# First rounds in another order, adapter loads and products later, a new warm-up and another last unit, in a retention-plus-adapters kernel

## The chip, the cores and the metric

The kernel runs on one core of one Trainium2 chip. A core has a matrix engine (TensorE, PE in the profile, its weight loads PEld), VectorE (DVE), ScalarE (ACT), GpSimd (POOL) and SyncE (SP), which work side by side and wait for each other through semaphores; transfers between the chip's main memory and the on-chip memory go through 16 DMA engines and are issued from an engine's queue, here mostly SP's. The metric is the device time of one execution in microseconds (us).

## The reference

The first half is a retention layer: attention scores without a softmax, weighted by a decay that depends on the distance and cut to the past. The second is a mixture of adapters on its output: each token picks the two best of eight experts, and their low-rank products are added.

```python
# q, k, v: (8 batches, 8 heads, 576 positions, 64), float32
scores = (1/sqrt(64)) * q @ k.T
rel = pos[:, None] - pos[None, :]
ret = scores * where(rel >= 0, gamma[h] ** rel, 0)       # gamma[h] = 1 - 2**(-5 - h)
x = (ret @ v).transpose(0, 2, 1, 3).reshape(4608, 512)

logits = x @ w_gate                                      # (4608, 8)
topk = the 2 largest logits of each token
w = softmax over those 2
out = x + sum over the 2: w * ((x @ A[e]) @ B[e])        # A: 512 x 16, B: 16 x 512
```

## The kernel before

**Units.** The 576 positions are cut into chunks of 128, with a last one of 64. A unit is one chunk of two batches (four batches for the last chunk): units 0 to 15 are full, four for each of four chunks, and 16 and 17 hold the last chunk. Units 0 to 3 belong to the first chunk and have no state from an earlier one. Within a unit, positions come as two blocks of 64 ("t = 0, 1"). From unit 2 to 15 ("paired"), q is loaded in another layout with longer runs.

**The decay** is split: k is multiplied by gamma to the power of minus its position and q by gamma to the power of its position times the scale (`scale_`, lines 162 to 184), on GpSimd, on VectorE, or half each. What is left of the mask is a 0/1 triangle, which `masks` (line 279) multiplies in while copying the scores out, four instructions for a unit in an order that is a parameter.

**Stages of a unit**, by the names that the order below uses, with the engine's lines:
- turn: `stage_T` and `evict_T` transpose k and q on TensorE (lines 215, 202) and copy the result out on ScalarE (240, 235). `shift_q` copies q's halves to the other partitions (252, 253).
- sums: `stage_U` forms k-transposed times v (300), `stage_A` adds it to the running state SP (332 to 335), `put` or `put_state` copies the state beside v (316).
- scores: `stage_S` (269) and the four masks (289). The first-chunk units copy only one half of q.
- products: `stage_X` multiplies masked scores, and q, with v, and with the state (350). In the first chunk the first half of it uses only the first 64 rows. `evict_x` copies the result, xT, out on ScalarE (366, 371).
- logits: `stage_Z` multiplies xT with AW, which holds A and w_gate (393), and copies to zs (406). choose: `routing_2` finds the best two on VectorE (416 to 421). `routing_3` is the sigmoid on ScalarE (431), which is the softmax over two. `routing_4` weights the small products on GpSimd (441, 443), into zc.
- small: `stage_P` and `evict_z` transpose zc (378, 386). back: `stage_B` transposes xT back (459). output: `stage_Y` adds the product with B (475), `evict_o` copies out (492), `store` writes.

**Order.** It is written out by hand: on each engine instructions run in the order in which the program issues them, and semaphores hold each one until its data and its buffer are ready. Loads are issued on SP's queue, units 0 to 5 ahead of everything, the later ones in `ahead(t)`, which also issues due stores, and, on GpSimd, copies the state for unit t + 1 and scales k and q of unit t + 2. Units 0, 1 and 2 run through their first stages one after the other (lines 575 to 628); then come rounds by hand (796 to 845), in which logits of unit 0 begin; from round 5 a loop (847) does scores(t), logits(t-1), small(t-2), choose(t-1), sums(t+1), turn(t+1), back(t-2), products(t), output(t-2). `finish` (693) handles the last units. Before, the order of the first units by hand on TensorE is, with the unit's number: ... scores 1, products 1, turn 2, sums 2, scores 2, logits 0, products 2, turn 3, sums 3, scores 3, logits 1, small 0, back 0, products 3, output 0, turn 4, logits 2, sums 4, scores 4, logits 3, small 1 and 2, back 1, output 1, sums 5, turn 5, back 2, products 4, output 2.

**Fills.** `fill_small` and `fill` run matmuls on zeros, ahead of the first data and where TensorE would wait in units 0 and 1.

**The adapter.** AW is loaded by four transfers of A and one of w_gate between the loads of unit 2 and unit 3 (lines 555 to 563), in runs of 64 and 32 bytes.

Of the kernel before, what the change touches and what calls it, by code (L numbers as in the profile page):

```python
# [18 lines left out]
def kernel(  # L19
# [115 lines left out]
    def load(u, w):  # L135
# [9 lines left out]
        elif w == "v":  # L145
            for t in range(2):
                hf = slice(64 * t, 64 * t + 64)
                nc.sync.dma_start(  # L148
                    out=block(u, t)[hf], in_=rows(w, 2 * bp, 2, s0 + 64 * t, 64)
                )  # L150
# [209 lines left out]
    def evict_x(u):  # L360
        st[u]["xT"] = []
        for b in range(2):
            xt = mo.tile([128, HP, 128], FP32, tag=f"xT{b}", name=f"xT{b}", bufs=3)
# [130 lines left out]
    def fill_small(n):  # L494
        pf = [pp.tile([128, 96], FP32, tag=f"o{r}", name=f"pf{r}") for r in range(2)]
        for _ in range(n):
            for c in range(2):
                for r in range(2):
                    sl = slice(64 * r, 64 * r + 64)
                    nc.tensor.matmul(  # L500
                        pf[r][64 * c : 64 * c + 64],
                        lhsT=zero[sl, 0:64],
                        rhs=zero[sl, 0:96],
                        start=True,
                        stop=True,
                        skip_group_check=True,
                    )

    def fill(n):
        if n == 0:  # L510
            return
        pf = pp.tile([128, 512], FP32, tag="o1", name="pf")
        for _ in range(n):
            nc.tensor.matmul(
                pf, lhsT=zero[:, 0:128], rhs=zero, start=True, stop=True, skip_group_check=True
            )

    o3 = out.rearrange("(b s) m -> b s m", s=S)

    def store(u):  # L520
        c, bp = units[u]
        of = st.pop(u)["osb"].rearrange("p b a o d -> p b (a o d)")
        for b in range(2):
# [4 lines left out]
            else:  # L528
                for t in range(2):
                    (nc.gpsimd if b and u == NU - 2 else nc.sync).dma_start(  # L530
                        out=o3[4 * bp + 2 * t + b, 128 * c : 128 * c + 64, :],
                        in_=of[64 * t : 64 * t + 64, b],
                    )


    def load_batch(u, w, b):
# [3 lines left out]
        )  # L540

# [13 lines left out]
    for dt in range(HP):  # L555
        nc.sync.dma_start(  # L556
            out=AW[:, dt, 0:ER].rearrange("p (e r) -> p e r", e=E),
            in_=moe_A[:, 128 * dt : 128 * dt + 128, :].rearrange("e d r -> d e r"),
        )
    nc.sync.dma_start(  # L560
        out=AW[:, :, ER : ER + E],
        in_=moe_w_gate.rearrange("(t p) e -> p t e", p=128),
    )
    for u in range(3, 6):
        for w in "kqv":
            load(u, w)

    both = (nc.gpsimd, nc.vector)
    pool2 = (nc.gpsimd, nc.gpsimd)
    dve2 = (nc.vector, nc.vector)  # L570
# [4 lines left out]
    fill_small(20)  # L575
# [8 lines left out]
    by_t = ((0, 0), (0, 1), (1, 0), (1, 1))  # L584
    for b, w, n in ((0, "k", 2), (0, "q", 1), (1, "k", 1), (1, "q", 0)):
        stage_T(0, w, (b,), "u" if w == "q" else "x")
        evict_T(0, w, b)
        fill(n)
# [24 lines left out]
    masks(1)  # L613
    scale_(2, "k", both)
# [12 lines left out]
    masks(2)  # L627
    scale_(3, "k", pool2)

    def ahead(t):  # L630
# [5 lines left out]
        if has(t + 1):  # L636
            first_state(t + 1)
        if has(t + 2):
            scale_(t + 2, "k", pool2)
            if t > 2:  # L640
                scale_(t + 2, "q", pool2)
# [51 lines left out]
    def finish():  # L693
# [16 lines left out]
        pz, zs, zc, po, osb = [], [], [], [], []  # L710
# [7 lines left out]
        for b in range(2):  # L718
            z = mo.tile([128, ER + E], FP32, tag=f"ze{b}", name="ze", bufs=1)
            m8 = mo.tile([128, E], FP32, tag=f"m8e{b}", name="m8e", bufs=1)  # L720
            ns = mo.tile([128, 1], FP32, tag=f"nse{b}", name="nse", bufs=1)
            ge = mo.tile([128, E], FP32, tag=f"gee{b}", name="gee", bufs=1)
            sg = mo.tile([128, E], FP32, tag=f"sge{b}", name="sge", bufs=1)
            cm = mo.tile([128, E], FP32, tag=f"cme{b}", name="cme", bufs=1)
            c = mo.tile([128, ER], FP16, tag=f"zce{b}", name="zce", bufs=1)
# [9 lines left out]
            )  # L735
            nc.scalar.activation(
                out=sg, in_=z[:, ER : ER + E], func=AFT.Sigmoid, bias=ns, scale=2.0
            )
            nc.gpsimd.tensor_tensor(out=cm, in0=ge, in1=sg, op=ALU.mult)
            nc.gpsimd.tensor_tensor(  # L740
                out=c.rearrange("p (e r) -> p e r", e=E),
                in0=z[:, 0:ER].rearrange("p (e r) -> p e r", e=E),
# [3 lines left out]
            zc.append(c)  # L746
            if b == 0:
                small(u - 1, "x0")
        back(u - 1)
        stage_Y(u - 1)  # L750
        evict_o(u - 1, (nc.scalar, nc.vector))
        store(u - 1)

        def small_b(b):
            p = pp.tile([128, 128], FP16, tag=f"u{b}", name="pzte")
            nc.tensor.matmul(
                p, lhsT=zc[b], rhs=ident16, is_transpose=True, start=True, stop=True
            )
            zt = mo.tile([128, 128], FP16, tag=f"zTe{b}", name="zTe", bufs=1)
# [3 lines left out]
        def output_b(b, zt):  # L763
            o = mo.tile([128, HP, 2, 64], FP32, tag=f"oe{b}", name="oe", bufs=1, align_bytes=256)
            for ho, eng in ((0, nc.scalar), (1, nc.vector)):
# [8 lines left out]
            of = o.rearrange("p a o d -> p (a o d)")  # L774
            for t in range(2):
                (nc.scalar if b and t else nc.sync).dma_start(
                    out=o3[4 * qd + 2 * t + b, 128 * c : 128 * c + 64, :],
                    in_=of[64 * t : 64 * t + 64],
                )

        zt0 = small_b(0)
# [119 lines left out]
```

## Time and profile before

| what | value |
|---|---|
| three runs | 190.16, 190.33, 191.59 us; median 190.33 |
| profiled execution | 190.79 us, of which the span of the profile is 188.9 us |
| TensorE busy | 167.3 us (89% of the span) |
| VectorE, ScalarE, GpSimd busy | 113.3, 114.1, 108.7 us |
| mean granted TensorE clock | 0.986 |
| moved by DMA | 38.99 MB, mean 206 GB/s |

A row of a timeline reads: start, length, engine, line, operation, output and inputs, count, and in brackets the engine's idle time before it with what ended it. An "issue" there is a wait for nothing that the profile can name. A row of the windows view gives, for a stretch of time, each engine's busy time with the count of instructions, then the granted clock of TensorE (1.00 is full), the share of time in which the DMA engines were busy, and GB/s. A row of the chain gives start, length, engine and tile. Rows of groups give busy time, mean length in ns, and idle time ahead of them.

### The profile page before, as it was taken

The page shows a single profiled execution, that of the slowest core. Times are in us where ns is not written, and L with a number is a line of the kernel's source. Part 1 is how long each engine was busy: PE and PEld are TensorE (multiplying, and loading weights), DVE is VectorE, ACT ScalarE, POOL GpSimd, SP SyncE. Part 2 cuts the span into 40 slices and gives each one's busy share as a digit, 9 for nine tenths or more (in the row PEclk, how much of TensorE's full clock was granted, in tenths as well). Part 3 has the DMA queues.
Part 4 walks back from the last instruction along what each step waited for, and adds up shares of the span by engine and source line. Part 5 has one row for each costly group of instructions (what it writes and reads, how often), then busy time and mean ns, then how long its engine had stood idle before and what let it go on. Part 6 is the DMA issues. An engine that isn't in the chain of part 4 may idle for free.

```text
span 188.9 us, 10441 instructions
## 1 busy us (share of the span) xinstructions
PE 167.3 (89%) x4675; PEld 148.9 (79%) x4675; DVE 113.3 (60%) x227; ACT 114.1 (60%) x255; POOL 108.7 (58%) x162
## 2 busy tenths in 40 slices
PE   3989598799889889898999999999997999999960
PEld 3578498588879788788999989899996988988840
DVE  1384837665296475748577787777594846555240
ACT  3437163735569484765767868494959394674650
POOL 1333321567769988493949586675969397520240
PEclk9999969999999999999999999999999999999998
DMA  7999969999999999999999999999998853112325
GB/s 157 248 221 225 227 70 232 202 224 246 224 228 235 262 252 277 252 260 247 241 257 246 266 232 250 221 278 226 271 206 243 181 169 115 50 68 111 115 56 166
DMA packets 108075, 38.99 MB, mean 206 GB/s; under 512 B 88768, under 2 KB 103488, under 8 KB 108032
## 3 DMA queue, kind: packets, MB, share of 16 engines
q1 hardware_dynamic: 107568, 37.71, 81.1%
q8 instruction: 36, 0.59, 1.4%
q0 software_dynamic: 240, 0.39, 1.0%
q10 hardware_dynamic: 224, 0.24, 0.5%
q14 instruction: 7, 0.06, 0.1%
HBM read 29.02 MB, written 9.44 MB: 204 GB/s over the span
## 4 chain that ended last, share of the span: by engine, by line
PE 59%; SPq 14%; issue 7%; DMA 6%; POOL 5%; DVE 4%; ACT 2%; POOLq 0%; ACTq 0%
PE px L350 15%; PE pz L393 12%; PE ps_s L269 8%; PE pu L300 6%; PE po L475 5%; PE po L459 4%; PE pt_k L215 4%; SPq L148 3%; SPq L556 3%; PE pt_q L202 3%; DMA k<-in_k_dram 3%; SPq L160 3%; DMA q<-in_q_dram 3%; POOL k L179 2%; SPq L538 2%
## 5 line engine op out<-in xcount | busy, mean ns | idle before, releaser
L179 POOL TENSOR_TENSOR k<-k,pack 128x512 f32<-128x512 f32 x32 | 34.9, 1109 | 17.4 <-DMA k<-in_k_dram 16.5
L350 PE MATMUL px<-x,v 128*64 128x64 f32 (+1 forms) x576 | 39.3, 226 | 2.6 <-DVE x L289 0.8
L289 DVE TENSOR_TENSOR x<-ps_s,pack 64x512 f32<-64x512 f32 (+1 forms) x38 | 25.1, 660 | 25.9 <-PE ps_s L269 25.6
L350 PE MATMUL px<-qT,v 128*64 128x64 f32 (+1 forms) x576 | 39.2, 226 | 1.3 <-DVE qT L289 1.1
L350 PEld LDWEIGHTS px<-x,v 128*64 128x64 f32 (+1 forms) x576 | 36.2, 140 | 4.4 <-ACT kT L240 1.0
L350 PEld LDWEIGHTS px<-qT,v 128*64 128x64 f32 (+1 forms) x576 | 36.1, 140 | 1.9 <-DVE qT L289 1.2
L393 PE MATMUL pz<-AW,xT 128*128 128x136 f32 x272 | 36.1, 286 | 0.6 <-ACT kT L240 0.6
L393 PEld LDWEIGHTS pz<-AW,xT 128*128 128x128 f32 x272 | 32.6, 190 | 1.8 <-ACT kT L240 0.8
L169 POOL TENSOR_TENSOR qs<-q,pack 128x512 f32<-128x512 f32 x25 | 26.1, 1062 | 4.1 <-DMA q<-in_q_dram 4.1
L406 ACT COPY zs<-pz 128x272 f32<-128x272 f32 x17 | 6.6, 386 | 33.2 <-PE pz L393 32.5
L289 DVE TENSOR_TENSOR qT<-ps_s,pack 64x512 f32<-64x512 f32 (+1 forms) x38 | 25.1, 660 | 1.1
L269 PE MATMUL ps_s<-qT,kT 64*64 64x64 f32 x1152 | 23.6, 224 | 2.1 <-issue 1.4
L269 PEld LDWEIGHTS ps_s<-qT,kT 64*64 64x64 f32 x1152 | 20.4, 137 | 6.2 <-issue 3.1
L441 POOL TENSOR_TENSOR cm<-ge,sg 128x16 f32<-128x16 f32 x17 | 4.0, 234 | 36.5 <-PE pt_k L215 16.9
L316 POOL COPY v<-SP 64x512 f32<-64x512 f32 x32 | 20.5, 640 | 1.6
L300 PE MATMUL pu<-v,k 64*64 64x64 f32 x1024 | 19.2, 221 | 0.8 <-DMA v<-in_v_dram 0.8
L240 ACT COPY kT<-pt_k 128x512 f32<-128x512 f32 x34 | 18.2, 589 | 1.2 <-PE pt_k L215 1.0
L253 DVE COPY x<-qT 64x512 f32<-64x512 f32 x17 | 14.5, 852 | 7.4 <-ACT qT L235 5.0
L366 ACT COPY xT<-px 128x512 f32<-128x512 f32 x28 | 16.3, 625 | 4.4 <-PE px L350 4.4
L300 PEld LDWEIGHTS pu<-v,k 64*64 64x64 f32 x1024 | 16.9, 134 | 2.5 <-DMA v<-in_v_dram 0.9
L492 ACT COPY osb<-po 128x512 f32<-128x512 f32 x33 | 17.6, 584 | 1.0 <-PE po L475 1.0
L252 DVE COPY x<-qT 64x512 f32<-64x512 f32 x14 | 8.1, 579 | 16.0 <-ACT qT L235 12.0
(68 smaller groups left out, 242.6 us busy)
## 6 DMA issues: line engine op xcount, KB each, us to landing
v<-in_v_dram SPq DMA_DIRECT2D x36, 256.0 KB, 5.2
q<-in_q_dram SPq DMA_DIRECT2D x34, 256.0 KB, 5.2
out_dram<-osb SPq DMA_DIRECT2D x32, 256.0 KB, 4.2
k<-in_k_dram SPq DMA_DIRECT2D x15, 512.0 KB, 5.7
k<-in_k_dram SPq DMA_DIRECT2D x6, 256.0 KB, 4.3
q<-in_q_dram SPq DMA_DIRECT2D x1, 512.0 KB, 6.9
out_dram<-oe SPq DMA_DIRECT2D x3, 128.0 KB, 3.3
AW<-in_moe_A_dram SPq DMA_DIRECT2D x4, 64.0 KB, 3.6
```

The lines of the kernel that those rows point to most:

```text
L169: engines[b].tensor_tensor(out=qs[:, :, 4 * b : 4 * b + 4, :].rearrange("p e h d -> p h e d"), in0=tl[:, b * H : b * H + H, :].rearrange(" ...
L179: engines[b].tensor_tensor(out=tl[:, b * H : b * H + H, :], in0=tl[:, b * H : b * H + H, :], in1=g[:, c, :].unsqueeze(2).broadcast_to((128 ...
L240: nc.scalar.copy(out=tl[:, r], in_=st[u]["p" + w][r])
L253: eng.tensor_copy(out=x2[0:64, 1, b], in_=qT[64:128, 1, b])
L269: nc.tensor.matmul(ps[ho][64 * t : 64 * t + 64, b, hp, :], lhsT=kT[sl, t, b, hp, :], rhs=qT[sl, t, b, hp, :], start=(hp == 0 and b == bs[0 ...
L289: nc.vector.tensor_tensor(out=out, in0=in0, in1=m, op=ALU.mult)
L300: nc.tensor.matmul(pu[t][64 * ho : 64 * ho + 64, b, hp, :], lhsT=kn[sl, h, :], rhs=block(u, t)[sl, h, :], start=(hp == 0 and b == 0), stop ...
L316: copy(out=dst[:, :, :, ho, :], in_=src[64 * ho : 64 * ho + 64])
L350: nc.tensor.matmul(px[b][64 * ho : 64 * ho + 64, hp, t, :], lhsT=block(u, t)[rw, b * H + 2 * hp + ho, :], rhs=facing(u, t, ho)[rw, b, hp, ...
L366: nc.scalar.copy(out=xt.rearrange("p a (t i e) -> p (a t) e i", t=2, e=2), in_=px.rearrange("p a t (e i) -> p (a t) e i", e=2),)
L393: nc.tensor.matmul(pz[:, b, :], lhsT=st[u]["xT"][b][:, dt, :], rhs=AW[:, dt, :], start=(dt == 0), stop=(dt == HP - 1), skip_group_check=True,)
L492: copy(out=s["osb"][:, :, :, ho, :], in_=s["po"][ho])
```

## The change

- The small quadrant matmuls of the warm-up become 64 matmuls over the whole array (`warmup`), and the fills are cut into narrower pieces (256 or 128 columns, the same number of columns in all).
- Unit 3's k, q and the first half of its v are loaded ahead of the adapter; the first transfer of A comes next, then the second half of that v, then the other four.
- The masks of units 1, 2 and 3 run in the order `by_t`, first half of the positions first. Fills of 4 and 2 (in units of 512 columns) stand ahead of products 1 and 2. k of unit 2 is scaled on GpSimd alone, k of unit 4 half on VectorE.
- Unit 3 runs through its first stages as units 1 and 2 do; logits 0 come only then. TensorE's order becomes: ... scores 1, fill, products 1, turn 2, sums 2, scores 2, fill, products 2, turn 3, sums 3, scores 3, logits 0, products 3, k of turn 4, q of turn 4, logits 1, small 0, back 0, output 0, sums 4, scores 4, logits 2, small 1, back 1, output 1, products 4, logits 3, small 2, turn 5, sums 5, back 2, output 2, and then the same loop. xT gets four buffers in place of three.
- In `finish`, the weighting of unit 17 moves from GpSimd to VectorE, its two batches are interleaved in another way with unit 16's output, which VectorE alone now copies out, while ScalarE copies out unit 17's; the stores of the last chunk go out as one transfer for each batch of a pair (of two blocks, 256 KB) in place of two.

```diff
-    def load(u, w):
+    def load(u, w, ts=(0, 1)):
...
-            for t in range(2):
+            for t in ts:
...
-            xt = mo.tile([128, HP, 128], FP32, tag=f"xT{b}", name=f"xT{b}", bufs=3)
+            xt = mo.tile([128, HP, 128], FP32, tag=f"xT{b}", name=f"xT{b}", bufs=4)
...
+    def warmup(n):
+        pf = pp.tile([128, 512], FP32, tag="o1", name="pf")
         for _ in range(n):
+            nc.tensor.matmul(
+                pf[:, 0:64], lhsT=zero[:, 0:128], rhs=zero[:, 0:64], start=True, stop=True,
...
+    def fill(n, w=256):
...
+        for _ in range(512 * n // w):
+                pf[:, 0:w], lhsT=zero[:, 0:128], rhs=zero[:, 0:w], start=True, stop=True,
...
-                for t in range(2):
-                    (nc.gpsimd if b and u == NU - 2 else nc.sync).dma_start(
-                        out=o3[4 * bp + 2 * t + b, 128 * c : 128 * c + 64, :],
-                        in_=of[64 * t : 64 * t + 64, b],
-                    )
+                nc.sync.dma_start(
+                    out=o5[bp, b, :, 128 * c : 128 * c + 64, :], in_=of[:, b]
+                )
...
+    def load_adapter(dt):
+        if dt < HP:
+            nc.sync.dma_start(
+                out=AW[:, dt, 0:ER].rearrange("p (e r) -> p e r", e=E),
...
+        else:
+            nc.sync.dma_start(
+                out=AW[:, :, ER : ER + E],
...
-    for dt in range(HP):
-        nc.sync.dma_start(
-            out=AW[:, dt, 0:ER].rearrange("p (e r) -> p e r", e=E),
...
-    nc.sync.dma_start(
-        out=AW[:, :, ER : ER + E],
...
-    for u in range(3, 6):
+    for w in "kq":
+        load(3, w)
+    load(3, "v", (0,))
+    load_adapter(0)
+    load(3, "v", (1,))
+    for dt in range(1, HP + 1):
+        load_adapter(dt)
+    for u in range(4, 6):
         for w in "kqv":
             load(u, w)
...
-    fill_small(20)
+    warmup(64)
...
-        fill(n)
+        fill(n, 128)
...
-    masks(1)
-    scale_(2, "k", both)
+    masks(1, None, by_t)
+    scale_(2, "k", pool2)
+    fill(4)
     stage_X(1)
...
-    masks(2)
+    masks(2, None, by_t)
     scale_(3, "k", pool2)
+    fill(2)
+    stage_X(2)
+    evict_x(2)
+    stage_T(3, "k", tag="s")
+    evict_T(3, "k")
+    scale_(3, "q", both)
+    stage_A(2)
+    stage_T(3, "q", tag="o")
+    evict_T(3, "q")
+    shift_q(3, nc.vector)
+    stage_U(3)
+    put_state(3, 1, st[3]["pu"][0], nc.scalar)
+    stage_S(3)
+    masks(3, None, by_t)
...
+    scale_(4, "k", both)
     ahead(2)
-    routing_4(0)
-    scores(3)
+    logits(0, "o0")
+    stage_X(3)
+    evict_x(3)
     stage_A(3)
     scale_(4, "q", both)
+    stage_T(4, "k", tag="s")
+    evict_T(4, "k")
+    choose(0)
+    routing_3(0)
+    routing_4(0)
+    stage_T(4, "q", tag="x")
+    evict_T(4, "q")
+    shift_q(4, nc.vector)
+    logits(1, "o0")
+    choose(1)
+    routing_3(1)
     ahead(3)
+    routing_4(1)
+    small(0, "u1")
     back(0)
     output(0)
+    sums(4)
+    put(4)
+    scores(4)
     logits(2, "x0")
...
+        choose_b(0)
+        sigmoid_b(0)
+        stage_P(u - 1, "x0")
+        choose_b(1)
+        evict_z(u - 1)
+        back(u - 1)
+        back_b(0, "s")
+        zt0 = weigh_b(0)
+        stage_Y(u - 1)
+        sigmoid_b(1)
+        back_b(1, "x")
+        output_b(0, zt0, (nc.scalar, nc.scalar))
+        zt1 = weigh_b(1)
+        evict_o(u - 1, (nc.vector, nc.vector))
+        store(u - 1)
+        output_b(1, zt1, (nc.scalar, nc.scalar))
```

160 lines of the change are left out of this document (58 added, 102 removed).

## Prediction

> **What bounds the kernel now.** I read the page's chain of waits first, then TensorE's busy time by stages, then the rows around each wait.
>
> ```profile
> PE 59%; SPq 14%; issue 7%; DMA 6%; POOL 5%; DVE 4%; ACT 2%; POOLq 0%; ACTq 0%
> ...
> 28.60:61.70 33.10, 29.73 (x798) 26.30 (x798) 21.10 (x44) 19.37 (x44) 21.28 (x30) 1.00 0.98 227
> 61.70:92.30 30.60, 27.23 (x791) 24.58 (x794) 19.06 (x36) 19.91 (x44) 22.26 (x32) 1.00 1.02 261
> 92.30:143.80 51.50, 51.37 (x1569) 47.68 (x1570) 37.74 (x72) 36.75 (x83) 37.73 (x54) 1.00 0.99 246
> ```
>
> In the chain TensorE has 59%. The columns of the last three rows are the stretch, its length, busy time of PE, PEld, DVE, ACT and POOL, the granted clock, the DMA share and GB/s. From 92.3 on TensorE never rests: a round takes 8.6 us (six in 51.5) and is nothing but matmul time, the same before and after. So the change can only earn in three places: the first rounds (up to 61.7, where round 5 begins with its scores), the stretch to 92.3, where TensorE rests 3.4 of 30.6 us, and the end.
>
> What TensorE waits for between 61.7 and 92.3 is not another engine (the chain of waits: start, length, piece):
>
> ```profile
> 68.64 0.66 issue
> 69.30 0.40 PE po L459 x7
> 69.70 2.02 PE px L350 x64
> 71.71 0.54 PE po L475 x4
> 72.26 0.96 PE ps_s L269 x53
> 73.22 0.35 issue
> ...
> q8 instruction: 36, 0.59, 1.4%
> ```
>
> Between two such stops lie 7 + 64 + 4 + 53 = 128 matmuls, with their weight loads 256 instructions; queue 8 brings code in 36 packets of 0.59 MB / 36 = 16 KB. The stops are waits for code, and they stand where the DMA share is 1.02. [...]
>
> **The change part by part: the start.** Warm-up and fills cover the wait for data. TensorE runs slowly at first: the 128x512 fills take 615 ns before 9.7 us and 382 ns at 15 to 17.
>
> ```profile
> L514 PE MATMUL pf<-zero 128*128 128x512 f16 x4 | 2.3, 615 | 0.0
> L514 PE MATMUL pf<-zero 128*128 128x512 f16 x3 | 0.8, 382 | 0.0
> ...
> 17.12 1.30 PE L300 MATMUL pu<-v,k 64*64 64x64 f32 x61
> 12.10 0.99 SPq L148
> ...
> v<-in_v_dram SPq DMA_DIRECT2D x36, 256.0 KB, 5.2
> ```
>
> A warmer array could end unit 0 about 1 us sooner. But unit 1's sums at 17.12 need v of unit 1, whose second half is issued at 12.10 (the chain of waits) and lands 5.2 later by v's median, at 17.3: they cannot move forward. Value **0**; bounds -0.3 and +1.0 (a warm-up that overruns, below).
>
> **Unit 1's products.** The masks by half let the first 64-row half of the products start after two masks in place of three.
>
> ```profile
> 19.54 0.68 DVE L289 TENSOR_TENSOR x<-ps_s,pack 64x512 f32<-64x512 f32 x1 [0.78 <-PE ps_s L269]
> 20.25 1.39 DVE L289 TENSOR_TENSOR qT<-ps_s,pack 64x512 f32<-64x512 f32 x2
> 21.67 0.69 DVE L289 TENSOR_TENSOR x<-ps_s,pack 64x512 f32<-64x512 f32 x1
> 22.40 0.27 PE L350 MATMUL px<-x,v 64*64 64x64 f32 x1 [0.38 <-issue]
> 20.00:23.40 3.40, 1.65 (x34) 1.31 (x34) 3.23 (x6) 0.00 (x0) 0.43 (x2) 0.99 1.08 208
> 23.40:26.80 3.40, 3.40 (x62) 3.28 (x62) 1.83 (x3) 1.55 (x3) 1.35 (x1) 0.50 0.63 64
> ```
>
> Masks 3 and 4 end at 22.36, so two masks earlier is 20.9. But the stop at 22.40 is put down to "issue": it is a wait for code, one block after that of unit 1's sums. By the instructions' order this border comes at the 475th matmul before, four into these products; after, warm-up, fills and units 0 and 1 hold 478 ahead of them, so it falls into the new fill, and the products still can't start before 22.4. Then all 64 are to do, not 60, behind three fills: **+0.4** (three fills of half the width at 0.1, from the 0.8 us of three whole ones less a drain, and four of 64 matmuls in 2.0). If code comes in time, they gain 22.4 - 20.9 = 1.5, the other bound. [...] The array ran at half clock for 3.4 us behind a stretch that held 1.65 us of matmul; after, the same stretch holds about 1.0, so I expect that half-clock stretch again, and its full effect is the bound +0.7.
>
> **Round order up to 61.7.** Before, logits 0 filled the wait for unit 2's masks:
>
> ```profile
> 29.50 2.12 PE L393 MATMUL pz<-AW,xT 128*128 128x136 f32 x16
> 32.10 0.27 PE L350 MATMUL px<-x,v 64*64 64x64 f32 x1 [0.47 <-ACT zs L406]
> 38.60 1.15 PE L269 MATMUL ps_s<-qT,kT 64*64 64x64 f32 x63
> ...
> 32.48 2.05 POOL L179 TENSOR_TENSOR k<-k,pack 128x512 f32<-128x512 f32 x2 [7.74 <-DMA k<-in_k_dram]
> 39.22 2.04 POOL L179 TENSOR_TENSOR k<-k,pack 128x512 f32<-128x512 f32 x2 [3.68 <-DMA k<-in_k_dram]
> 35.79 1.07 ACT L240 COPY kT<-pt_k 128x512 f32<-128x512 f32 x2 [0.38 <-PE pt_k L215]
> ```
>
> After: unit 2's scores end at about 30.0 (0.4 behind the 29.6 where logits 0 take over); four masks of 0.69 end at 32.8; the second half of the products (1.0) ends at 33.8, with a fill of 0.4 in the gap. k of unit 3 no longer waits behind the adapter (it was scaled from 32.48), so its transposes follow; ScalarE sets the pace with xT's second copy, kT and qT (0.6 + 1.07 + about the same) to 36.6; scores 3 end at 37.7, where they ended at 39.75 before; logits 0 (2.05) end at 39.75. **The same work is done at the same moment**: what unit 3's early loads give (its k by some 6 us), the bare wait for masks takes back.
>
> From there: products 3 wait for masks 3 (40.5) and end at 41.8; k of unit 4 has landed at 39.2 as before, is transposed by 42.45. On VectorE stand behind masks 3: half of k 4 (to 41.2), two state sums (to 42.6), half of q 4 (to 43.3); q's transposes wait for that, 0.85 us, and behind them logits 1. Logits 1 end at 45.85; output 0 could follow at 46.8, but its zT stands on ScalarE's queue behind sigmoid 1, and that behind choose 1 and the shift of q 4 on VectorE: 48.05 at my count, 1.25 us.
>
> ```profile
> 57.54 0.64 PE pt_k L215 x16
> 58.19 0.50 PE pt_q L202 x16
> ```
>
> What is left to round 5 is output 0 (0.54), then two rounds of 8.6 less one pair of these transposes (1.14), one scores (1.1) and one products (2.02), and 0.25 for output 1's zT: 0.54 + 17.2 - 4.26 + 0.25 = 13.7. That gives **61.8**, against 61.7 before: value **0**. Without any of these waits it would be 1.9 earlier: the lower bound; the upper one is +1.7, half of a half-clock stretch of 3.4. Moving the border between blocks of code (it now falls into sums 5) makes the next stop end at about 59.7 + 4.3 = 64.0, the 4.3 being the distance from 69.30 to 73.57 above; before, it ended at 63.6 (the row below). **+0.4**.
>
> ```profile
> 63.60 0.33 PE L269 MATMUL ps_s<-qT,kT 64*64 64x64 f32 x4 [0.78 <-issue]
> ```
>
> **The loads.** SP issues the adapter's five small transfers in one row, and the DMA engines run dry:
>
> ```profile
> 19.77 6.30 SPq L556 DMA_DIRECT2D AW<-in_moe_A_dram  x4
> 26.74 0.51 SPq L160 DMA_DIRECT2D k<-in_k_dram  x1
> 24.60:28.60 4.00, 3.85 (x122) 3.54 (x124) 0.79 (x2) 3.29 (x7) 0.15 (x1) 0.73 0.70 81
> ```
>
> 4.0 us at 81 GB/s, where 246 is usual, are 2.7 us lost. After, one of the four large ones stands between the halves of v 3, the others still stand together ahead of unit 4: I take a quarter, **-0.7**, in loads from unit 4 on and so in the stops up to 92.3; bounds 0 and -2.7. POOL takes over half of k 2 from VectorE (1.04 more on POOL, done by 21.3, hidden). The fourth xT buffer costs nothing: logits 0 come two units later.
>
> **The end.** Before, weights go over POOL and both engines copy out:
>
> ```profile
> 179.83 0.21 POOL L739 TENSOR_TENSOR cme<-gee,sge 128x8 f32<-128x8 f32 x1 [2.73 <-ACT sge L736]
> 180.12 0.40 POOL L740 TENSOR_TENSOR zce<-ze,cme 128x128 f16<-128x128 f32 x1
> 181.67 1.18 SPq L530 DMA_DIRECT2D out_dram<-osb  x2
> 182.96 2.25 SPq L776 DMA_DIRECT2D out_dram<-oe  x3
> ```
>
> On VectorE a weighting costs, at my estimate from its masks (0.69 for 512 columns), 0.2 + 0.3 in place of 0.21 + 0.08 + 0.40, but the first stands behind choose 1 (0.5). ScalarE copies all four halves, so the last copy ends at about 184.0, 0.5 later than before; unit 16's output waits on VectorE until about 183.7, 2 us later. SP's last issue ends at 184.9 in place of 185.2, with 256 KB in it in place of 128. Value **-0.1**; bounds -0.6 and +0.5.
>
> **Sum.** 0 + 0 (unit 1's +0.4 is inside the 61.8) + 0.4 - 0.7 - 0.1 = -0.4. The profiled execution took 190.8 us (span 188.9), so 190.4; the median of the runs, 190.33, is 0.46 below it: **190.0**.
>
> **Rivals.**
> - *Loads and code come in time* (faster): interleaving keeps the DMA engines full, all 2.7 us come back, and unit 1's half-masks work. Round 5 then begins 1.9 earlier, and a third of the 3.4 us of stops goes: -2.9 in all, **187.3**. For it: 81 GB/s is a hole, and SP issues nothing else in it. Against: three of four transfers still stand together.
> - *Half clock* (slower): the bare waits ahead of products 2 and of q 4's transposes each hold little matmul. One stretch of 3.4 us at clock 0.50 costs 1.7, and both 3.4: 190.0 + 3.4 = **193.4** (one alone, 191.7, stays within the forecast's range). It decides when a stretch of 3.4 us holds less than about 1.65 us of matmul, as the one from 20.0 did. For it: logits 0 no longer stand there; against: fills of 0.9 and 0.4 do.
> - *The warm-up overruns* (slower): 64 loads of 128 columns one after another at the fill's cold 108 ns take 6.9 us from 1.2 on, to 8.1, where unit 0 was ready at 4.98. Of the 3.1 us the wait for v 1 hides about 1.1 and q 4 about 0.85: +1.2, **191.2**.
>
> ```profile
> L514 PEld LDWEIGHTS <-zero 128*128 128x128 f16 x4 | 0.3, 108 | 0.4
> 4.98 0.69 PE L215 MATMUL pt_k<-pack,k 64*128 64x64 f32 x8 [1.98 <-DVE k L179]
> ```
>
> [...]
>
> **How the numbers follow.** Forecast 0.41 (188.6 to 191.8, its own bounds at half their size), faster rival 0.33, both half-clock stretches 0.20, overrun 0.04, other losses 0.02. A measurement here tells 1% (188.4 to 192.2) from no change: faster 0.33, same 0.41 + 0.04 = 0.45, slower 0.20 + 0.02 = 0.22. The range reaches from just below the fast rival to between one and two half-clock stretches: 187.0 to 192.9.
>
> **What would show it.** Right: unit 1's products begin at 22.4 with an idle time put down to issue; scores 3 end near 37.7; round 5's scores begin at 61 to 62; stops marked issue remain up to about 90. Wrong: products 1 from 21.0; k 4 scaled before 37; a clock of 0.50 beyond 27 us; a first transpose after 6 us.

## The result: 11% slower, and where the time went

| | before | after |
|---|---|---|
| median of the runs (lowest to highest) | 190.67 us (190.16 to 191.59) | **212.33 us** (210.63 to 214.56) |
| ratio, 95% interval | | **1.11** [1.1003, 1.1198] |
| profiled execution, span | 188.9 us | 212.6 us |
| mean granted TensorE clock | 0.986 | 0.923 |

The forecast was 190.0 us, in a range of 187.0 to 192.9. In this document ratios are taken from undisturbed executions alone, medians and lowest to highest from all of them, so a kernel whose executions scatter can have a ratio near 1 and a higher median; the profiled execution of after, 214.56 us, is the slowest of its four and not among the undisturbed, so its profile shows more loss ahead of the end than the others can have had.

The mean clock of after, 0.923, counts its last 22 us, in which the rows below give 0.50 and TensorE has no work; only some 5 us of full clock (half of 6.83 + 3.41) were lost while it worked.

The span is cut first at the start of round 5's scores (61.67 and 67.15 us) and at the end of TensorE's last matmul (183.1 and 188.54). The windows view of before (stretch, length, busy time of PE, PEld, DVE, ACT and POOL with counts, granted clock, DMA share, GB/s):

```profile
10.00:61.67 51.67, 45.27 (x1294) 39.91 (x1292) 32.84 (x65) 28.90 (x62) 26.99 (x36) 0.97 0.96 211
61.67:183.10 121.43, 115.15 (x3243) 104.45 (x3242) 77.56 (x156) 81.48 (x186) 79.24 (x118) 1.00 0.79 206
```

The same of after, and its last 22 us:

```profile
10.00:67.15 57.15, 48.57 (x1297) 43.24 (x1289) 28.98 (x60) 28.59 (x60) 25.48 (x33) 0.91 0.98 219
67.15:188.54 121.39, 115.40 (x3243) 104.38 (x3242) 81.39 (x163) 80.56 (x186) 78.58 (x115) 1.00 0.75 193
190.00:195.00 5.00, 0.00 (x0) 0.00 (x0) 0.00 (x0) 0.00 (x0) 0.00 (x0) 0.51 0.13 41
195.00:212.60 17.60, 0.00 (x0) 0.00 (x0) 0.00 (x0) 0.00 (x0) 0.00 (x0) 0.50 0.12 47
```

In these two executions the middle has not moved: 121.43 and 121.39 us. **The first rounds are 5.5 us longer**: 45.27 us of matmul time have become 48.57 (+3.3), and 6.40 us of rest 8.58 (+2.2). **Behind the last matmul 24.1 us pass where 5.8 passed before**: +18.3. Behind the last copy, which ends at 189.12, no engine computes anything; all that runs is DMA, at 41 to 47 GB/s.

What runs there is the four merged stores. Their issues (timeline of after, SP's and ScalarE's queues), and the DMA view of after from 186 to 213 us:

```profile
187.95 0.66 SPq L801 DMA_DIRECT2D out_dram<-oe  x1
188.72 5.66 SPq L524 DMA_DIRECT2D out_dram<-osb  x2
189.15 1.13 ACTq L801 DMA_DIRECT2D out_dram<-oe  x1
```

```profile
DMA  0000011111111111111111111111111111111000
q1 hardware_dynamic: 390, 0.79, 8.2%
q10 hardware_dynamic: 130, 0.26, 2.5%
```

The same view of before, from 181 to 189 us, where the same 1.05 MB leave in eight transfers of 128 KB, some of them through a third queue:

```profile
DMA  0000000005991979899978779978962000000000
GB/s 0 0 0 0 0 0 0 0 0 143 225 236 51 246 195 236 195 287 348 307 225 266 266 277 297 348 205 225 348 226 82 10 0 0 0 0 0 0 0 0
q1 hardware_dynamic: 400, 0.66, 26.7%
```

The digits are tenths of the 16 DMA engines' time. In before most stand at 7 to 9 until all has left; in after there is an even 1, and the windows above give it as 0.12 to 0.13. Two engines of sixteen are 0.125. The trace's semaphore events set these transfers apart too (issue, first and last step, number of steps; this kernel's earlier stores have 16 each, and so has each of the eight at the end of before):

```
187.95  oe,  batch 0   first 189.00  last 197.90   3 steps
188.72  osb, first     first 189.68  last 206.48   3 steps
189.15  oe,  batch 1   first 190.36  last 204.79   3 steps
189.31  osb, second    first 194.80  last 211.61   3 steps
```

The transfer's pattern is (t, b fixed, 64 rows, 512 columns), and its slowest dimension t has 2 entries; in the eight separate stores it is the 64 rows. The two DMA views also count 8 packets under 512 B with the four merged stores, 2 for each, and 128 with the eight of before, 16 for each. From the share, the steps and these packets I read that a merged store kept 2 of the 16 engines busy, and that the 2 entries of t are the reason. No row names an engine, so this is my estimate; the experiments below test the second half of it.

The first rounds, in the windows view of after, cut where the granted clock changes:

```profile
5.77:22.83 17.06, 13.33 (x418) 10.99 (x416) 10.10 (x19) 8.13 (x18) 6.68 (x8) 1.00 1.10 239
19.40:22.80 3.40, 1.52 (x26) 0.92 (x20) 2.58 (x4) 0.23 (x1) 2.04 (x2) 1.00 1.21 230
22.83:29.66 6.83, 6.83 (x154) 6.48 (x152) 2.29 (x4) 3.22 (x6) 3.97 (x4) 0.50 0.94 212
36.50:39.90 3.40, 0.55 (x36) 0.41 (x29) 0.42 (x1) 1.10 (x3) 1.04 (x1) 1.00 0.88 221
39.90:43.31 3.41, 3.41 (x82) 3.29 (x80) 1.20 (x2) 1.16 (x2) 1.04 (x1) 0.50 0.94 214
```

And the waits of TensorE in after, 10 to 68 us (engine, tile, what was waited for: us in all, times, longest):

```profile
PE pu L300 <- issue: 4.0, 2, 2.8
PE pf L507 <- issue: 1.9, 1, 1.9
PE po L459 <- issue: 0.4, 1, 0.4
```

The same waits of before:

```profile
PE ps_s L269 <- issue: 0.8, 1, 0.8
PE px L350 <- issue: 0.4, 1, 0.4
```

I read the two longest stops as waits for code: 1.9 us in the new fill, from 20.3 to 22.15, and 2.8 us in unit 3's sums, from 36.9 to 39.8. The times of the code packets in the trace agree: one lands at 20.57 and one at 38.24, and TensorE goes on 1.6 and 1.5 us later. Each stop leaves a stretch of 3.4 us with little matmul in it (1.52 and 0.55 us), and behind each TensorE runs at half clock, for 6.83 and 3.41 us. Before, there was one such stretch of 3.4. Half of the 6.83 us more at clock 0.50 is 3.4, which is the +3.3 of matmul time. The stops marked issue are 6.3 us in place of 1.2; other waits have become shorter, so that 2.2 us more of rest are left.

The 5.5 us are not the usual size. The kernel with stores cut by columns (below) is the same program up to the last unit; in its profiled execution, of 211.51 us, round 5 begins at 64.44, and the last matmul ends at 184.01, only 0.9 us later than before.

### The profile page after: what moved, and what is told of

Its sections match the earlier page's. It is cut to its first block, busy times and chain, and to the rows that moved or that the text cites. A ratio compares the mean times of both kernels' runs of the same rounds, so it can differ in the third digit from the quotient of the medians.

```text
span 212.6 us, 10460 instructions
## 1 busy us (share of the span) xinstructions
PE 171.8 (81%) x4686; PEld 154.4 (73%) x4686; DVE 114.1 (54%) x230; ACT 113.8 (54%) x256; POOL 106.6 (50%) x156
## 4 chain that ended last, share of the span: by engine, by line
PE 69%; issue 6%; ACT 6%; DVE 5%; DMA 2%; POOL 0%; SPq 0%; ACTq 0%; POOLq 0%
PE px L350 18%; PE pz L393 14%; PE ps_s L269 10%; PE pu L300 8%; PE po L475 4%; PE pt_k L215 4%; PE pt_q L202 3%; PE po L459 3%; DMA q<-in_q_dram 2%; DVE qT L289 2%; DVE x L289 1%; PE pf L507 1%; ACT sg L431 1%; ACT kT L240 1%; PE pt_q L215 1%
## 5 line engine op out<-in xcount | busy, mean ns | idle before, releaser
L350 PE MATMUL px<-x,v 128*64 128x64 f32 (+1 forms) x576 | 40.0, 228 | 1.5 <-ACT kT L240 0.9
L350 PE MATMUL px<-qT,v 128*64 128x64 f32 (+1 forms) x576 | 39.8, 228 | 0.3 <-DVE qT L289 0.3
L350 PEld LDWEIGHTS px<-x,v 128*64 128x64 f32 (+1 forms) x576 | 36.8, 142 | 3.8 <-ACT kT L240 1.4
L350 PEld LDWEIGHTS px<-qT,v 128*64 128x64 f32 (+1 forms) x576 | 36.6, 142 | 0.8 <-DVE qT L289 0.4
L393 PE MATMUL pz<-AW,xT 128*128 128x136 f32 x272 | 36.7, 289 | 0.0
L393 PEld LDWEIGHTS pz<-AW,xT 128*128 128x128 f32 x272 | 33.2, 193 | 1.2
L300 PE MATMUL pu<-v,k 64*64 64x64 f32 x1024 | 20.4, 227 | 4.1 <-issue 4.0
L300 PEld LDWEIGHTS pu<-v,k 64*64 64x64 f32 x1024 | 17.8, 140 | 6.1 <-issue 4.7
L316 POOL COPY v<-SP 64x512 f32<-64x512 f32 x32 | 20.3, 633 | 1.6
L253 DVE COPY x<-qT 64x512 f32<-64x512 f32 x17 | 15.2, 894 | 8.9 <-ACT qT L235 6.3
L240 ACT COPY kT<-pt_k 128x512 f32<-128x512 f32 x34 | 18.2, 586 | 1.5 <-PE pt_k L215 1.4
L252 DVE COPY x<-qT 64x512 f32<-64x512 f32 x14 | 9.3, 666 | 17.4 <-ACT qT L235 13.4
L492 ACT COPY osb<-po 128x512 f32<-128x512 f32 x32 | 17.0, 583 | 1.5 <-PE po L475 1.5
```

Source lines behind the costliest of these rows:

```text
L240: nc.scalar.copy(out=tl[:, r], in_=st[u]["p" + w][r])
L253: eng.tensor_copy(out=x2[0:64, 1, b], in_=qT[64:128, 1, b])
L300: nc.tensor.matmul(pu[t][64 * ho : 64 * ho + 64, b, hp, :], lhsT=kn[sl, h, :], rhs=block(u, t)[sl, h, :], start=(hp == 0 and b == 0), stop ...
L316: copy(out=dst[:, :, :, ho, :], in_=src[64 * ho : 64 * ho + 64])
L350: nc.tensor.matmul(px[b][64 * ho : 64 * ho + 64, hp, t, :], lhsT=block(u, t)[rw, b * H + 2 * hp + ho, :], rhs=facing(u, t, ho)[rw, b, hp, ...
L393: nc.tensor.matmul(pz[:, b, :], lhsT=st[u]["xT"][b][:, dt, :], rhs=AW[:, dt, :], start=(dt == 0), stop=(dt == HP - 1), skip_group_check=True,)
```

## The experiments

The kernels were measured in six groups, each on one chip beside the kernel before. The medians of the kernel before are 191.46 us (beside the stores and the last unit), 194.23 (the first rounds, unless another is named), 191.35 (the number of instructions), 193.35 (the two side by side), 193.86 (the two behind them) and 194.72 (fills on top). They differ by up to 1.8%, so each kernel is compared with the one beside it.

### The stores

**Split again.** The changed kernel with the last chunk's stores cut by blocks (unit 16's are shown, unit 17's are cut in the same way):

```diff
-                nc.sync.dma_start(
-                    out=o5[bp, b, :, 128 * c : 128 * c + 64, :], in_=of[:, b]
-                )
+                for t in range(2):
+                    nc.sync.dma_start(
+                        out=o5[bp, b, t, 128 * c : 128 * c + 64, :],
+                        in_=of[64 * t : 64 * t + 64, b],
+                    )
...
```

> The changed kernel, with the last chunk's stores cut again into one transfer for each block of 64 rows (SP for unit 16 and for the first batch of unit 17, ScalarE's queue for its second). Theory A (the merged stores are what takes the 18 us after the last instruction: a transfer whose outermost dimension is the 2 blocks runs on 2 of the 16 DMA engines): 194 to 196 us, the last store lands within 3 us of its issue, and about 5 us of the loss stay, all ahead of round 5. Theory B (the weighting on VectorE and the later output of unit 16 hold the end up): 208 or more.

Measured: 194.23 us median (191.06 to 201.57, 10 runs), ratio to before 1.0028 [0.9973, 1.0082]. By the medians 18.1 us of the 21.7 are gone, though on another chip; by the ratios, 1.11 and 1.0028, nearly all is. The executions scatter over 10 us. Each of the eight stores now has 16 semaphore steps. The 5 us that were expected to stay ahead of round 5 don't show in the ratio.

**Cut the other way.** The same number of transfers of the same 128 KB, but cut by columns, so that t stays the slowest dimension:

```diff
-                nc.sync.dma_start(
-                    out=o5[bp, b, :, 128 * c : 128 * c + 64, :], in_=of[:, b]
-                )
+                for m in (slice(0, 256), slice(256, 512)):
+                    nc.sync.dma_start(
+                        out=o5[bp, b, :, 128 * c : 128 * c + 64, m], in_=of[:, b, m]
+                    )
...
```

> The changed kernel, with each of the four merged stores cut into two transfers by columns, 128 rows by 256 columns each: as many transfers and bytes as in the split by blocks, but the 2 blocks stay the outermost dimension. Theory A (2 engines by that dimension): still 210 us or more, with some packets more for the same bytes. Theory B (256 KB in one transfer are too many): 194 to 197, as with the split by blocks.

Measured: 212.21 us (209.55 to 216.65), 20.8 above before on its chip. Its DMA view from 184 to 210 us:

```profile
DMA  0111111111111111111111111111111111111000
q1 hardware_dynamic: 780, 0.79, 9.2%
```

Eight transfers of 128 KB, as in before, and the time is that of four of 256 KB. It is neither the size nor the number. This kernel differs from the one above in the slowest dimension, and in runs of 1 KB in place of 2 KB; but the four merged stores have runs of 2 KB and are as slow. Each of the eight has 3 semaphore steps here, against 16 there.

**The merged stores alone**, in the kernel before:

```diff
...
-            for t in range(2):
-                (nc.scalar if b and t else nc.sync).dma_start(
...
+            (nc.scalar if b else nc.sync).dma_start(
+                out=o5[qd, b, :, 128 * c : 128 * c + 64, :],
...
```

> The kernel before, with nothing changed but the last chunk's stores, merged to one transfer for each batch of a pair. Theory A: 15 to 20 us slower than before, 206 to 211 (a little less than the changed kernel's loss behind the end, since unit 16's stores start 6 us earlier here). Theory B (merging costs nothing by itself): 190 to 191.

Measured: 209.68 us (208.28 to 211.43), ratio 1.097 [1.0898, 1.1042]; 18.2 us above before on its chip. Its four stores have 3 steps each too. Added or taken away, the merging is worth some 18 us.

### The last unit

**The new order of `finish` alone**, in the kernel before, with separate stores:

> The kernel before up to the last unit, with the changed kernel's order of the last unit (weighting on VectorE, unit 16 copied out by VectorE, unit 17 by ScalarE) and stores split by blocks. By the prediction's term for the end (-0.1, bounds -0.6 to +0.5): 190.0 to 191.2. If the order of the last unit costs by itself, 192 or more. The difference to the changed kernel with split stores is then what the first rounds cost; the trace has 5.5 us of it at the start of round 5.

Measured: 192.99 us (192.68 to 194.04), ratio 1.013 [1.0074, 1.0185]. The end of unit 16's and 17's copies, in the timeline of this kernel:

```profile
182.76 0.17 DVE L748 TENSOR_TENSOR cme<-gee,sge 128x8 f32<-128x8 f32 x1 [0.82 <-ACT sge L741]
182.97 0.29 DVE L749 TENSOR_TENSOR zce<-ze,cme 128x128 f16<-128x128 f32 x1
183.34 1.29 DVE L492 COPY osb<-po 128x512 f32<-128x512 f32 x2
184.50 0.65 ACT L781 COPY oe<-poe 128x256 f32<-128x256 f32 x2 [0.38 <-PE poe L777]
185.18 1.23 ACTq L786 DMA_DIRECT2D out_dram<-oe  x2
185.27 1.41 SPq L531 DMA_DIRECT2D out_dram<-osb  x2
```

and in before:

```profile
181.43 0.40 POOL L740 TENSOR_TENSOR zce<-ze,cme 128x128 f16<-128x128 f32 x1
182.20 1.12 POOL L530 DMA_DIRECT2D out_dram<-osb  x2 [0.37 <-issue]
182.96 1.57 SPq L776 DMA_DIRECT2D out_dram<-oe  x2
183.10 0.42 DVE L770 COPY oe<-poe 128x256 f32<-128x256 f32 x1 [0.49 <-PE poe L766]
183.62 0.56 ACTq L776 DMA_DIRECT2D out_dram<-oe  x1
```

The weighting is shorter, 0.17 + 0.29 us for 0.21 + 0.40. But products 17 end at 178.66 here and at 177.51 before; from there to the last copy are 6.49 us for 6.02, and from the last copy to the end of the span 6.05 for 5.37, since unit 16's stores, which had left from 181.67 on through two queues, now follow behind 185.27. That is +1.15 us or 0.6%, just below the interval. The rest, products 17 being late already, lies ahead of the lines that this edit touches, and stays unexplained.

### The first rounds

All kernels of this part have the last unit and the stores of the kernel before.

**The first rounds alone**: warm-up, fills, masks by half, loads' order and rounds of the changed kernel.

> The changed kernel with the last unit and all stores of the kernel before: only the first rounds, the loads' order, the masks by half and the warm-up are new. Split stores alone gave a median of 194.2 us with a spread of 191.1 to 201.6; the last unit's order cost 1.15 us behind products 17 (6.49 for 6.02 to the last copy, 6.05 for 5.37 from there to the end). Theory A (the first rounds lose to half-clock stretches of 3.41 us, whose number differs from one execution to the next): the same spread 1.1 us lower, 190 to 200, median 193. Theory B (the first rounds lose a fixed time, the two stops for code of 1.9 and 2.9 us): 195 with a spread under 2 us. Theory C (the first rounds lose nothing, and the whole loss lies in the stores): the time of the kernel before, within 1 us.

Measured: 196.59 us (194.27 to 200.75, 12 runs; before 194.23), ratio 1.0107 [1.0049, 1.0166]. The spread is that of theory A.

**A longer fill ahead of unit 1's products**:

```diff
-    warmup(64)
+    warmup(54)
...
-    fill(4)
+    fill(10, 512)
```

> The same, with 54 warm-up matmuls in place of 64 and ten fills of 512 columns in place of eight of 256 ahead of unit 1's products: the code border moves 8 instructions on, out of the fills, and TensorE is busy to about 21.7 us where it stopped at 20.3. Theory A (the half-clock stretch at 22.8 us follows on a window with too little matmul work): the stretch at 22.8 goes, the products of unit 1 take 2.2 us in place of 3.7, the spread falls under 3 us, and the median is 188 to 190. Theory B: the stop for code comes whatever stands ahead of it and is as long (until 22.2 us or later), so nothing moves: the median of the first-rounds kernel within 1 us.

Measured: 196.51 us (192.09 to 200.9), ratio 1.0018 [0.9949, 1.0086]. The profiled execution had no half-clock stretch ahead of its last matmul. The place in question:

```profile
19.40:22.80 3.40, 2.69 (x21) 1.14 (x15) 2.58 (x4) 0.14 (x1) 2.03 (x2) 1.00 1.17 265
22.80:29.70 6.90, 5.20 (x208) 4.86 (x211) 2.50 (x4) 3.63 (x7) 2.36 (x2) 1.00 0.92 205
```

2.69 us of matmul in place of 1.52, and the clock stays at 1.00. Yet the median is that of the kernel without the fill, and the intervals of the two ratios overlap, so no gain is shown: stops for code of 1.1 and 1.3 us come further on, and the mean clock of other executions of this kernel goes down to 0.961.

**The adapter's loads ahead of unit 3's**, as before the change:

```diff
-    for w in "kq":
-        load(3, w)
-    load(3, "v", (0,))
-    load_adapter(0)
...
+    for dt in range(HP + 1):
+        load_adapter(dt)
+    for u in range(3, 6):
```

> The first-rounds kernel with the adapter loads ahead of unit 3's, as before the change. If the adapter loads beside it are what makes the code packet of the sums of unit 3 late (asked for at about 32.5, landed at 38.2 us, a stop of 2.85 us), the stop falls under 1 us, the half-clock stretch at 39.9 goes, and the median is 2 to 4 us lower than the first-rounds kernel's. If the packet is late for another reason, the stop stays over 2 us and the median is within 1 us of it, or up to 1.5 us longer because unit 3's loads land later.

Measured: 198.14 us (193.42 to 203.33, 6 runs). In its profile the stop in unit 3's sums is gone, but one of 1.4 us stands in scores, and the first one takes 2.46 us. When a packet was asked for, no row shows. No gain shows from either order: inconclusive.

**The masks of units 1 to 3 as before** (`masks(1)` for `masks(1, None, by_t)`):

> The first-rounds kernel with the masks of units 1 to 3 in whole blocks in the old order. If masking by half lets products start earlier, this one is 0.3 to 1.0 us slower than the first-rounds kernel. If code or loads hold TensorE at these places, it is the same within 0.3 us.

Measured: 193.11 us (190.22 to 197.72; before 191.35), ratio 1.0056 [1.0005, 1.0108]. It is not slower than with masks by half (1.0107, on another chip); those earn nothing that shows.

**Fills in the kernel before**, ahead of unit 1's products:

```diff
-    fill_small(20)
+    fill_small(18)
...
+    fill(8)
     stage_X(1)
```

> The kernel before with 8 warm-up matmuls less and 8 fills of 512 columns ahead of unit 1's products, where TensorE stood for 0.77 and 1.10 us (19.5 to 21.7). If too little matmul work there calls the half-clock stretch at 23.4 to 26.8 us, the stretch goes, and the median is 0.7 to 1.7 us below the kernel before (189 to 190). If it comes whatever fills the stop, the time is that of the kernel before within 0.5 us, or 0.5 us longer for the fills.

Measured: 194.35 us (191.57 to 196.83), ratio 0.9955 [0.9906, 1.0004]: just undecided. In its profile the half-clock stretch has moved on, to 32.12.

### Is it the number of instructions?

In both kernels queue 8 brings code in packets of 16 KB, one behind the other (36 in before, 37 in after), so I thought the new order might be paced by it. Three kernels tested that.

**Less code in the kernel before** (`fill(4)` for `fill_small(20)`, the warm-up as long):

> The kernel before with 4 warm-up matmuls of 128x512 in place of 80 of 64x96: nearly the same busy time (1.7 us at half clock for 1.8), 152 instructions less. A code packet is 16,384 bytes for about 270 started instructions, and the kernel before takes 53.8 us for ten of them between 8.2 and 62.1 us, 5.4 us each. Theory A (the first rounds are paced by the arrival of code, one packet behind the other): 152 instructions are 0.56 of a packet, so the fifth round's scores come up to 3.0 us earlier, and 1 to 2.5 us of it arrive at the end: ratio 0.987 to 0.995. Theory B (paced by the loads and by TensorE's own work): the stops only change place, ratio 0.997 to 1.003.

Measured: 191.71 us (189.16 to 194.38), ratio 1.0001 [0.9955, 1.0048]. No gain.

**More code in the kernel before** (`fill_small(36)`):

> The opposite: the kernel before with 144 warm-up matmuls of 64x96 in place of 80, 128 instructions more; they take 1.5 us in the 1.98 us in which TensorE waited for the first scaled block, so they cost no time themselves. Theory A (paced by the arrival of code): 0.47 of a packet, so up to 2.5 us longer, ratio 1.005 to 1.013. Theory B: ratio 0.997 to 1.003.

Measured: 193.29 us (191.03 to 202.99), ratio 1.0099 [1.0052, 1.0147]. Slower, as the code theory has it, but alone it doesn't carry it.

**Less code in the first-rounds kernel**: `fill(8, 512)` for `warmup(64)`, and all fills 512 columns wide.

> The first-rounds kernel with all its fills and the warm-up made of 512-column matmuls: 148 instructions less, the warm-up 3.5 us as before. Theory A: the stops for code of the first rounds (1.27, 0.54, 1.03 and 0.47 us in its profile) shrink by half or more, the fifth round's scores come 2 to 3 us earlier, and the time is 1 to 2.5 us below the first-rounds kernel's, about that of the kernel before. Theory B: within 0.5 us of the first-rounds kernel.

Measured: 192.35 us (189.22 to 204.16), ratio 0.9989 [0.9941, 1.0038].

Both kernels once more, side by side on one chip:

> The first-rounds kernel (last unit and stores of the kernel before) once more, on one chip with the kernel of few instructions. It gave 1.0107 [1.0049, 1.0166] of the kernel before on one chip, and the kernel of few instructions gave 0.9989 [0.9941, 1.0038] on another. If the number of instructions is the cause (code paces the first rounds of the new order), this one comes 1 to 3 us above the next; if the two chips made the difference, within 0.7 us.

> The first-rounds kernel with fills and warm-up of 512 columns, 148 instructions less, on the same chip as the one above. Theory A (code paces the new order): 1 to 3 us below it, ratio to the kernel before 0.993 to 1.003. Theory B (the chip made the difference): within 0.7 us of the one above.

Measured: 199.25 us (195.2 to 203.11), ratio 1.0168 [1.0086, 1.0251], and 194.03 us (192.66 to 196.69), ratio 1.0025 [0.9972, 1.0078]. The intervals don't meet: the edit of warm-up and fills takes away the loss of the first rounds. The first of the two, in the windows view:

```profile
8.50:11.90 3.40, 1.47 (x46) 1.07 (x42) 2.83 (x8) 0.65 (x2) 0.40 (x1) 1.00 0.86 190
11.90:18.70 6.80, 6.26 (x140) 6.03 (x142) 3.15 (x6) 2.33 (x4) 3.18 (x3) 0.50 0.81 185
22.10:25.50 3.40, 1.34 (x43) 0.96 (x35) 2.73 (x5) 0.58 (x1) 2.88 (x3) 1.00 1.17 228
25.50:32.30 6.80, 6.80 (x119) 6.03 (x121) 1.93 (x3) 2.47 (x5) 2.74 (x3) 0.50 0.92 201
```

It has 13.6 us at half clock, each stretch behind one with 1.3 to 1.5 us of matmul; the second kernel's profile has 6.8.

But the edit changes two things, the number of instructions and the width of the fills. **Wide fills and much code** (`fill_small(18)` and `fill(5, 512)` as the warm-up):

> The first-rounds kernel of few instructions (1.0025 and 0.9989 of the kernel before) with 72 small quadrant matmuls in front of 5 wide ones as its warm-up, in place of 8 wide ones: the same length to 0.3 us, wide fills elsewhere, but 132 instructions more, so 16 less than the first-rounds kernel (1.0168 and 1.0107). If the number of instructions made the difference: 1.008 to 1.018. If the wide, dense fills did (more matmul work in each 3.4 us, fewer half-clock stretches): 0.997 to 1.005.

Measured: 194.72 us (192.34 to 197.33; before 193.86), ratio 0.997 [0.9926, 1.0013]. **Narrow fills and less code** (`warmup(20)`):

> The first-rounds kernel with 20 warm-up matmuls in place of 64, its fills narrow as they were: 88 instructions less, but TensorE then stands from 2.3 to 5.1 us. If the number of instructions makes the difference: 0.998 to 1.008. If dense work does: 1.010 to 1.020, with half-clock stretches as before or more.

Measured: 194.71 us (191.69 to 196.69), ratio 0.9992 [0.994, 1.0043]. Neither theory is borne out: here much code is not slow, and narrow fills are not. What these three variants have in common is that the 64 narrow matmuls over the whole array are not in front. But that this warm-up is the cause isn't shown: the last two ran without the long one beside them, on another chip, and other kernels with such a warm-up came to 1.0018 (54 in front, with a longer fill), 1.0056 (masks as before) and 1.0028 (the changed kernel with split stores).

### Fills on top

**Fewer warm-up matmuls and fills in the kernel before**:

```diff
-    fill_small(20)
+    fill(4)
...
+    fill(8)
     stage_X(1)
```

> The kernel before with 4 wide warm-up matmuls and 8 fills of 512 columns ahead of unit 1's products. The fills alone (with 80 warm-up matmuls become 72) gave 0.9955 [0.9906, 1.0004]. If the two stops of 0.77 and 1.10 us there, with the half-clock stretch behind them, are what can be had in the old order, 0.990 to 0.996; if the stops for code only move on to the next border, 0.997 to 1.005.

Measured: 193.23 us (191.96 to 194.41; before 194.72), ratio 0.9954 [0.9899, 1.0008].

**Ten fills in the first-rounds kernel of few instructions**:

> The first-rounds kernel of few instructions with 10 fills of 512 columns ahead of unit 1's products in place of 4, which cover 1.3 us more of the time in which its code is on the way. If the half-clock stretches behind the stops are what is left of its loss, ratio 0.990 to 0.998; if the fills only add their 1.3 us, 1.004 to 1.010.

Measured: 195.87 us (193.16 to 196.08), ratio 1.0052 [0.9983, 1.012]: nothing gained. Two kernels with eight fills in the old order came out at 0.9955 and 0.9954, both intervals ending just above 1. No version shown here beats the kernel before beyond its interval.

## Why the prediction was wrong, point by point

- **The end (-0.1, bounds -0.6 to +0.5): wrong, by 18 us.** This is the failed step. Its words were "SP's last issue ends at 184.9 in place of 185.2, with 256 KB in it in place of 128": the merged store was priced by its issue and its bytes, and its way through the DMA engines was taken as it had been. The runs showed a DMA share of 0.12 to 0.13 and 3 semaphore steps in place of 16, and 24.1 us behind the last matmul in place of 5.8. The access pattern in the diff has t = 2 in the first place, as all three kernels here that are slow behind the end have (after, the column cut, the merged stores alone). The bounds came from engine work alone, and no rival had a transfer in it. The rest of the step was nearly right: I put the last copy 0.5 later, and from products 17 to the last copy it was 6.48 for 6.02. But the stores of unit 16, 2 us later at my count, were given no price: with separate stores they leave 0.68 us more behind the last copy.
- **Round order up to 61.7 (0, bounds -1.9 to +1.7): wrong in the profiled executions.** In the one of after round 5 begins at 67.15, in that of the column cut at 64.44. In after, scores 3, forecast to end at 37.7, ended at 42.09. The step counted waits for masks and for ScalarE; what it left out is a code border, whose stop of 2.8 us stands in unit 3's sums. It had priced the border in sums 5 (0.4), but not this one. How much of it reaches the end is not shown: in the column cut 0.9 us did.
- **Unit 1's products (+0.4): right in where they begin**, at 22.58 (forecast 22.4), held by code, in the new fill, and the half-clock stretch came behind it as expected. It took 6.83 us, not 3.4. The turn of unit 2 behind these products begins at 26.21 in place of 25.27, 0.9 later, so the upper bound of +0.7 was too small.
- **The half-clock rival (193.4): right in its mechanism and size in the profiled execution, wrong in its trigger.** Its 3.4 us for two more stretches are the 3.3 measured. It looked for them in waits for masks; they came behind stops for code, at 1.52 and 0.55 us of matmul in 3.4, which agrees with the 1.65 that it named as the point. Over all runs that is no sharp point: half clock also came behind 2.16 and 2.20 us of matmul (split stores, masks as before) and not behind some windows with 1.50 to 1.83.
- **The start (0), and the overrun rival (191.2): no overrun.** The 64 pairs took 3.59 us, to 4.78, so their weight loads overlap: 56 ns a pair for a load of 132. The first transposes came at 5.2. Unit 1's sums began at 17.23, held by v, as forecast. Whether such a warm-up goes with more half-clock stretches later on stays open (below).
- **The loads (-0.7): came earlier, gained nothing that shows.** k of unit 4 landed at 37.9 in place of 39.2, and the hole stays: 90 GB/s from 30.4 to 34.2. With the adapter first the time was no clearer either way. The faster rival that was built on this step has a small slip: its 1.9 and a third of 3.4 are 3.0, not 2.9; it decides nothing.
- Of the signs named, three of the "wrong" ones did not come (products 1 from 21.0, k 4 scaled before 37, a first transpose after 6), and one did: a clock of 0.50 beyond 27 us. Of the "right" ones, the start of products 1 and the stops marked issue were seen; the end of scores 3 and the start of round 5 were not.

Without the merged stores the forecast of no change to speak of holds: 1.0028 for the changed kernel with split stores. The first rounds alone came to 1.0107 and 1.0168, the last unit alone to 1.013, and 0.997 to 1.0025 is had in the same rounds with another warm-up. So no gain of the new order shows. A loss of 1% in the first rounds or in the last unit isn't established for the whole change, since 1.0028 holds both.

**What stays open.** Whether a warm-up that ends at 4.8 us changes the half-clock stretches later on. With 54 or 64 narrow matmuls in front the profiled executions have 0 to 13.7 us at half clock, in the same rounds without them 0 to 10.2: the two overlap. The number of instructions, the width of the fills and the length were each changed with something else, and no pair of runs isolates a cause.

## What to carry to other kernels

Before two transfers are merged, read the slowest dimension of the new pattern on both sides: here the larger stores with 2 there had a DMA share of 0.12 to 0.13 and took 23.7 us, the smaller ones with 64 took 6.0, and at the very end of a kernel nothing hides it. Where TensorE waits for code, count the instructions to the next stop for the new order as well, in every stage that it touches (in before the stops at 68.64 and 73.22 are 128 matmuls with 128 weight loads apart), and price a stop with the half-clock stretch that may follow it (6.83 and 3.41 us in after), not by its own length alone. When a change bundles parts, its smallest line can be the one that decides.

## What the runs showed of the hardware

- 1.05 MB in four stores whose slowest dimension has 2 entries left at 41 to 47 GB/s, with a DMA share of 0.12 to 0.13, and took 23.7 us from first issue to last landing (187.95 to 211.61 in after); in eight stores with 64 rows there they took 6.0 (181.67 to 187.69 in before).
- In these runs half-clock stretches came behind windows of 3.4 us with 0.55 to 2.20 us of matmul. No sharp point shows: windows with 1.50 (adapter first, from 153.81), 1.74 (fills on top, from 146.68) and 1.83 us (the second of the two side by side, from 40.22) had none behind them, nor had the one with 2.69. A stretch lasted 3.41 us or two, three times that.
- Stops marked issue, read here as waits for code, stood between 10 and 68 us in every one of these orders: the longest was 0.8 us in before, 0.5 with 20 warm-up matmuls, 2.8 in after and 3.4 with the column cut, and their place moved with the edits of the fills.
- 64 weight loads of 128x128 in a row, each 132 ns long in the profile and each with a matmul of 64 columns, followed each other every 56 ns (after, 1.19 to 4.78 us).
